# Attention in plain fp32 on half and quarter tiles of TensorE in place of split operands on whole tiles

## The chip, the cores and the metric

The kernel runs on one core of a Trainium2 chip. That core has TensorE (PE in the profile, PEld for its weight loads), VectorE (DVE), ScalarE (ACT), GpSimd (POOL) and SyncE (SP, which issues DMAs). The metric is the device time of one execution in microseconds. Before the change it is 808.48 us, the median of 3 runs.

## The reference

Attention with rotary embedding over 2 batches of 8 heads, 576 tokens, 64 numbers per head, and behind it a gated feed-forward layer and a mixture of four experts on the 1152 tokens. Everything is fp32.

```python
q_rot, k_rot = (rotate(q), rotate(k))          # [2, 8, 576, 64]
scores = matmul(q_rot, k_rot.T) / sqrt(64)
attn = exp(scores - max(scores)); attn = attn / (sum(attn) + 1e-09)
x = matmul(attn, v)                            # -> [1152, 512]
xn = x / sqrt(mean(x * x) + 1e-06) * rms_g
g, val = xn @ w_gate, xn @ w_val               # 512 -> 1536
x = (silu(g) * val) @ w_out                    # 1536 -> 512
out = sum over 4 experts of p[:, e] * (relu(x @ w1[e]) @ w2[e])   # 512 -> 1024 -> 512
```

## The kernel before

**Operands.** The fast matmul type of the program is float32r. So that nothing is lost, each fp32 operand is held as a rounded part and a remainder ("hi" and "lo"), and a product is made of the parts that matter: three passes in the layers behind attention (PASSES), and in attention by stacking hi and lo on the 128 partitions, since a head has only 64 numbers.

**Stages.** Attention runs over 8 pairs of heads, pairs 0 to 3 for the first batch and 4 to 7 for the second. Then come the gate and value products (L805), the output product (L868), and for each expert its first layer (w1_unit, L931) and second layer (w2_group, L964).

**One pair.** Queries and keys are loaded and rotated (rotate, L446 to L452), split (split_hi, split_lo L500, v_hi, v_lo) and transposed on PE (q_or_k L525, k_left L535, q_left L547), with an evacuation of each transpose out of PSUM (evac, L511 to L515). s_tile makes the scores of 128 queries of one head against 576 keys: four float32r matmuls of 288 columns (L577), nine such steps in a pair (the ninth takes the 64 left-over queries of both heads, with eight matmuls). top takes the maximum on DVE (L583), expo the exponential on ACT (L588). t_tile, t_left, t_keys and t_corner transpose the exponentials on PE (L613, L629, L622, L636); parts evacuates each twice, hi on ACT (L606) and lo on DVE (L607). pv multiplies with the values: nine matmuls of 288 columns for each head and half of the queries (L652), folded over two halves of the partitions (L179 on ACT, L660 on DVE). scale_main and scale_left (L686, L697) divide by the sums.

**Around it.** The weights of the later layers are loaded, joined and split during pairs 4 to 7 (w_first, w_join L328 and L329, w_parts L368 and L369). gv_early makes gate and value products of the first batch while attention of the second is running: 16 groups of twelve matmuls, one PSUM bank each. The norm of the first batch (rms_mean L732, five plain fp32 matmuls a call; rms_spread L767; rms_apply) stands in pair 5.

**What sets the order.** The kernel is recorded, not scheduled: each step has a place, 9 for a pair plus a number from the tables POS, POS0, POSB, POS1 (and an engine from ENG and its like), and run() issues all steps sorted by place. Each engine then works through its own instructions in that order. PSUM has two buffers of two banks for scores ("big") and four of one bank for the rest ("one").

Of the kernel before, what the change touches and what calls it, by code (L numbers as in the profile page):

```python
# [8 lines left out]
F32 = mybir.dt.float32  # L9
# [12 lines left out]
    "load_k": -14.3442, "load_q": -13.3903, "rot_k0": -12.4, "rot_q0": -8.066,  # L22
    "rot_k1": -12.39, "rot_q1": -8.056, "rot_k2": -12.38, "rot_q2": -8.046, "rot_k3": -12.37, "rot_q3": -8.036,
    "sqadd": 15.77, "k_hi": -6.2198, "k_lo": -5.49, "q_hi": -5.473, "q_hi2": -4.604, "q_lo": -4.48, "kA": -3.592,
    "kLA": -4.0692, "qA0": -1.45, "qA1": -2.3793, "qB0": 1.5567, "qB1": 0.1894, "qL": 1.9708, "kB": 2.3,
    "kLB": 2.35, "qk_evac": 0.0223, "load_v": -3.3, "v_hi": 4.5018, "v_lo": 5.5461, "S": 0.1146, "top": 0.0456,
    "exp": 1.0525, "T": 2.2, "T_left": 7.9119, "T_corner": 6.2219, "T_keysA": 6.2256, "T_keysB": 11.3022,
    "hi": 0.0135, "lo": 0.8261, "pvA0": 8.9935, "pvA1": 9.4029, "pvB0": 12.6577, "pvB1": 13.5, "fold1": 0.2017,
    "fold2": 0.7357, "recip": 12.2577, "spread": 13.4482, "scale": 15.3215, "scale_left": 14.2785,
    "scale2": 0.0703, "squares": 15.7612, "mean": 1.3, "rspread": 4.8093, "apply": 5.5685,  # L30
    "apply_hi": 0.3766, "apply_lo": 0.5069,
    "w_first": [37.0005, 39.9382, 43.081, 45.3845, 48.8978, 50.7319, 54.1549, 55.9597, 79.06, 82.6],
    "w_join": [37.4505, 40.3882, 43.5310, 45.8345, 49.3478, 51.1819, 54.6049, 56.4097, 79.08, 82.7],
    "w_parts": [39.7348, 41.4602, 45.9122, 47.5214, 51.0007, 53.2283, 56.7202, 57.6825],
# [13 lines left out]
    "T_left": 7.9259, "pvA1": 9.8703, "T_corner": 5.9941,  # L48
    "gv_out": 0.2708, "lo": 0.4192, "recip": 11.4284, "pvB0": 13.0091,
}  # L50

POSB = {
# [3 lines left out]
}  # L56
ENGB = {"rot_k0": "v", "rot_k1": "v", "rot_k2": "v", "rot_k3": "v"}
POS7 = {
   
}  # L60
# [35 lines left out]
def attention_moe_kernel(ctx, tc, q, k, v, w_gate, w_val, w_out, rms_g, probs, w1, w2, rope, out):  # L96
# [63 lines left out]
    def lookup(name, base, first, second, last):  # L160
# [5 lines left out]
        for t in tables if pair == 0 or pair >= NPAIR else [base]:  # L166
            if name in t:
                return t[name]
# [1077 lines left out]
```

## Time and profile before

| | us |
|---|---|
| median of 3 runs | 808.48 |
| lowest, highest | 808.05, 809.56 |
| span of the profiled execution | 806.9 |
| first score matmul (L577) starts | 10.17 |
| first matmul of the output product (L868) starts | 251.70 |

Up to 251.7 us the core does attention and the gate and value products of the first chunk; from there to the end it does the output product, the other chunks and the experts. The profile gives each engine's busy time; on PE a matmul's bar includes its latency and bars overlap, so what one matmul costs in a run is read from the start of one to the start of the next. The mean of a group of short instructions on ACT or DVE likewise contains latency that the next instruction overlaps.

### The profile page before, as it was taken

The page shows a single profiled execution, that of the slowest core. Times are in us where ns is not written, and L with a number is a line of the kernel's source. Part 1 is how long each engine was busy: PE and PEld are TensorE (multiplying, and loading weights), DVE is VectorE, ACT ScalarE, POOL GpSimd, SP SyncE. Part 2 cuts the span into 40 slices and gives each one's busy share as a digit, 9 for nine tenths or more (in the row PEclk, how much of TensorE's full clock was granted, in tenths as well). Part 3 has the DMA queues.
Part 4 walks back from the last instruction along what each step waited for, and adds up shares of the span by engine and source line. Part 5 has one row for each costly group of instructions (what it writes and reads, how often), then busy time and mean ns, then how long its engine had stood idle before and what let it go on. Part 6 is the DMA issues. An engine that isn't in the chain of part 4 may idle for free.

```text
span 806.9 us, 13012 instructions
## 1 busy us (share of the span) xinstructions
PE 780.0 (97%) x4994; PEld 732.7 (91%) x4994; DVE 475.5 (59%) x883; ACT 397.5 (49%) x784; POOL 400.5 (50%) x320
## 2 busy tenths in 40 slices
PE   7899988899999999999999999999999999999997
PEld 6799877799998999999999899898989989898996
DVE  6899988977778765621286445445444444444442
ACT  4899988788565554213344334243333424333330
POOL 5777886672100066414436455555554555555440
PEclk9899999899999999999999999999999999999999
DMA  4011322230134433300000020110202011020002
GB/s 127 18 48 47 99 82 84 84 96 1 54 105 132 131 103 107 105 1 27 26 28 27 27 79 27 52 54 26 79 2 79 27 53 53 27 79 1 1 27 91
DMA packets 41805, 46.64 MB, mean 58 GB/s; under 512 B 7568, under 2 KB 34960, under 8 KB 41744
## 3 DMA queue, kind: packets, MB, share of 16 engines
q1 hardware_dynamic: 41744, 45.82, 18.3%
q8 instruction: 39, 0.64, 0.3%
q14 instruction: 22, 0.18, 0.1%
HBM read 43.45 MB, written 2.36 MB: 57 GB/s over the span
## 4 chain that ended last, share of the span: by engine, by line
PE 82%; DVE 7%; ACT 6%; issue 2%; POOL 1%; SPq 0%; DMA 0%; ACTq 0%; DVEq 0%; POOLq 0%
PE o L964 24%; PE o L931 22%; PE b L805 12%; PE o L868 9%; PE b L577 3%; PE o L652 3%; PE o L525 2%; PE o L613 2%; PE o L805 2%; ACT PP L588 1%; ACT PTA L606 1%; PE o L622 1%; DVE PTA L607 1%; ACT AR L179 1%; DVE nm L583 1%
## 5 line engine op out<-in xcount | busy, mean ns | idle before, releaser
L951 POOL TENSOR_TENSOR PTA<-PP,PTA 128x1152 fp32r<-128x1152 f32 x32 | 85.9, 2684 | 101.3 <-ACT PP L950 100.8
L964 PE MATMUL o<-QK,PTA 128*128 128x512 f32 x513 | 128.4, 389 | 0.0
L805 PE MATMUL b<-XN,WS 128*128 128x384 f32 (+1 forms) x768 | 126.5, 325 | 0.9 <-DVE PP L817 0.7
L805 PEld LDWEIGHTS b<-XN,WS 128*128 128x128 f32 x768 | 125.4, 188 | 1.5 <-DVE PP L817 1.3
L964 PEld LDWEIGHTS o<-QK,PTA 128*128 128x128 f32 x513 | 96.1, 188 | 19.8
L931 PE MATMUL o<-XN,WS 128*128 128x288 f32 x768 | 112.2, 295 | 0.0
L931 PEld LDWEIGHTS o<-XN,WS 128*128 128x128 f32 x768 | 105.7, 188 | 0.5
L384 POOL TENSOR_TENSOR WS<-RAW,WS 128x512 fp32r<-128x512 f32 x64 | 72.9, 1167 | 39.6 <-ACT WS L383 37.0
L949 ACT ACTIVATE PTA<-PP 128x1152 fp32r<-128x1152 f32 x32 | 37.4, 1168 | 106.2 <-DVE PP L944 106.2
L820 POOL TENSOR_TENSOR PTA<-PP,PTA 128x384 fp32r<-128x384 f32 x24 | 29.8, 1240 | 118.7 <-ACT PTA L819 118.7
L931 PE MATMUL o<-XT,WS 128*128 128x288 f32 x576 | 86.6, 295 | 0.0
L972 DVE SCALAR_TENSOR_TENSOR X<-o,pr,X 128x512 f32<-128x512 f32 x63 | 46.7, 749 | 64.9 <-PE o L964 64.9
L931 PEld LDWEIGHTS o<-XT,WS 128*128 128x128 f32 x576 | 79.8, 188 | 0.0
L383 ACT ACTIVATE WS<-RAW 128x512 fp32r<-128x512 f32 x64 | 32.5, 566 | 79.2 <-DVE RAW L391 79.2
L868 PE MATMUL o<-PTA,QK 128*128 128x288 f32 (+1 forms) x396 | 64.1, 305 | 0.8 <-ACT X L873 0.8
L607 DVE TENSOR_TENSOR PTA<-o,PTA 128x512 fp32r<-128x512 f32 (+2 forms) x96 | 61.3, 648 | 4.9 <-ACT PTA L606 3.9
L868 PEld LDWEIGHTS o<-PTA,QK 128*128 128x128 f32 x396 | 58.8, 188 | 1.0 <-ACT X L873 1.0
L583 DVE TENSOR_REDUCE nm<-b 128x1 f32<-128x576 f32 x72 | 54.1, 751 | 9.6 <-PE b L577 8.7
L606 ACT ACTIVATE PTA<-o 128x512 fp32r<-128x512 f32 (+2 forms) x96 | 53.5, 567 | 7.3 <-PE o L629 2.1
L937 DVE TENSOR_TENSOR PP<-o,PP 128x288 f32<-128x288 f32 x32 | 14.6, 457 | 71.9 <-ACT PP L936 65.6
L588 ACT ACTIVATE PP<-b,nm 128x576 f32<-128x576 f32 x72 | 53.4, 742 | 4.9 <-DVE nm L583 4.5
L817 DVE TENSOR_TENSOR PP<-b,PP 128x384 f32<-128x384 f32 (+1 forms) x32 | 17.0, 531 | 64.3 <-ACT PP L816 64.2
(184 smaller groups left out, 1449.3 us busy)
## 6 DMA issues: line engine op xcount, KB each, us to landing
RAW<-in_moe_w_dram SPq DMA_DIRECT2D x16, 512.0 KB, 3.4
AR<-in_moe_w_dram SPq DMA_DIRECT2D x16, 512.0 KB, 3.6
RAW<-in_moe_w_gate_dram SPq DMA_DIRECT2D x6, 512.0 KB, 3.5
RAW<-in_moe_w_val_dram SPq DMA_DIRECT2D x6, 512.0 KB, 3.4
AR<-in_moe_w_out_dram SPq DMA_DIRECT2D x6, 512.0 KB, 3.6
AR<-in_moe_w_gate_dram SPq DMA_DIRECT2D x5, 512.0 KB, 3.5
AR<-in_moe_w_val_dram SPq DMA_DIRECT2D x5, 512.0 KB, 3.4
AR<-in_v_dram SPq DMA_DIRECT2D x8, 256.0 KB, 3.4
```

What stands on the lines that cost most here:

```text
L384: eng.tensor_sub(dst(1), src, f32(dst(0)))
L583: nc.vector.tensor_reduce(nm[:, bufi, j : j + 1], box[0][:, :, 0:HS], axis=AX.XY, op=ALU.max, negate=True)
L588: nc.scalar.activation(pp(pair, j).rearrange("p (n t) -> p n t", n=2), box[0][:, :, 0:HS], AF.Exp, bias=nm[:, bufi, j : j + 1], scale=1.0, ...
L606: at(time + when("hi"), lambda: nc.scalar.activation(hi, view(box[0]), AF.Copy))
L607: at(time + when("lo"), lambda: nc.vector.tensor_sub(lo, view(box[0]), f32(hi)))
L805: nc.tensor.matmul(ps[:, 0:n], lhsT=w[:, lw, d, :], rhs=XN[:, lx, d, tok], start=(i == 0), stop=(i == 3 * ND - 1))
L868: nc.tensor.matmul(ps[:, 0:n], lhsT=w[:, lw, d * P : (d + 1) * P], rhs=hb(f, lx, tok), start=(i == 0), stop=(i == 11))
L931: nc.tensor.matmul(ps, lhsT=w[:, lw, a, k, :], rhs=xs(b, lx, k, c), start=(i == 0), stop=(i == 5))
L949: nc.scalar.activation(hi, q, AF.Relu)
L951: nc.gpsimd.tensor_sub(lo, q, f32(hi))
L964: nc.tensor.matmul(ps, lhsT=hb(f, lx, slice(t * P, (t + 1) * P)), rhs=w[:, lw, :], start=(i == 0), stop=(i == 11),)
L972: nc.vector.scalar_tensor_tensor(OA[:, t, :], in0=ps, scalar=p, in1=OA[:, t, :], op0=ALU.mult, op1=ALU.add)
```

## The change

Attention is done in plain fp32. Nothing is split: split_hi, split_lo, q_again, v_parts, the tiles QK, V2, QLZ and both evacuations of parts are gone.

- turn transposes the rotated keys or queries of both heads of a pair, in ten transposes of 64 partitions each, with one evacuation. Afterwards one head stands on partitions 0 to 63 and the other on 64 to 127 (KQ), and two DMAs from SBUF to SBUF (dup) write each head to the other half too (KQ2).
- s_step makes the scores of 128 queries of one head in two matmuls of 288 columns, one on each half of the partitions (left-over queries: four, on quarters). In the first two steps of pair 0 both heads are done at once from KQ alone.
- t_tile transposes in 8 or 10 pieces of 64 partitions and evacuates once (evac, mostly ACT); t_left has three evacuations.
- pv works on quarters of the array: 64 keys by 64 numbers of a head, 18 matmuls for both heads of one half of the queries, in three places (two, two and one key chunks). The two halves of the keys land in two banks, added by pv_out on ACT and pv_add on DVE.
- PSUM: "two" and "acc" are single buffers of two banks (transposes of the exponentials in the one; turn, pv, scale and gv_early in the other) until turn_over, after the last pair, swaps them for four buffers of one bank.
- gv_early evacuates gate and value together. The rope table is loaded from the ACT queue. All places in the tables are new.

```diff
 POS = {
-    "load_k": -14.3442, "load_q": -13.3903, "rot_k0": -12.4, "rot_q0": -8.066,
+    "load_k": -12.18, "load_q": -12.0135, "load_v": -0.6939, "rot_k0": -10.5625, "rot_k1": -9.0157, "rot_k2": -8.4013,
...
+    def turn(time, pair, m, eng):
+        x = turned[m]
...
+            box.append(ps_two(acc))
+            for i in range(5):
+                for r in range(2):
+                    a = HALF[r]
...
+                    nc.tensor.transpose(box[0][:, 1 - r, c : c + 64], x[a, o : o + P], ident[a, a])
...
+            nc.sync.dma_start(out=y[HALF[1], o : o + a.stop - a.start], in_=x[HALF[0], a])
+            nc.sync.dma_start(out=y[HALF[0], b], in_=x[HALF[1], b])
...
+            for n in range(2):
+                for i in (h,) if t < 4 else range(2):
+                    rows, c = (slice(0, P), cols) if t < 4 else (HALF[i], slice(576 - 576 * i, 640 - 576 * i))
                     nc.tensor.matmul(
-                        box[0][:, n, 0:HS], lhsT=lhsT, rhs=QKV[:, 2, h, cols],
-                        start=(i == 0), stop=(i == len(todo) - 1),
+                        box[0][rows, n, 0:HS], lhsT=queries(pair, i, c, n == i), rhs=keys(pair, i, n, n == i),
+                        start=True, stop=True,
                     )
...
+    def t_tile(time, pair, h, t, eng):
...
+            box.append(ps_two())
+            for i in range(nk):
+                for r in range(2):
+                    a, o = HALF[r], (ks.start + i) * P
+                    nc.tensor.transpose(box[0][:, r, 64 * i : 64 * i + 64], pp(pair, t)[a, o : o + P], ident[a, a])
...
-        at(time + when("hi"), lambda: nc.scalar.activation(hi, view(box[0]), AF.Copy))
-        at(time + when("lo"), lambda: nc.vector.tensor_sub(lo, view(box[0]), f32(hi)))
...
+            for k in ks:
+                for h in range(2):
+                    for r in range(2) if k < 4 else (h,):
+                        i = 4 if k == 4 else 5 * h + k
+                        nc.tensor.matmul(
+                            box[0][HALF[h], r, 0:HS], lhsT=VN[HALF[r], pair % 2, i, :],
+                            rhs=PT[pair % 2][HALF[r], i, cols], start=(k == 0), stop=(k == (4 if h == r else 3)),
+                        )
```

On PE, about the middle of an early pair, it stood before like this (L577 scores, L613 and L629 transposes of exponentials, L525 of queries and keys, L652 the value product):

```order
L577 MATMUL b_670<-QK 128x288 x4
L613 MATMUL o_677<-ident,PP 128x128 x4
L525 MATMUL o_683<-ident,XN 128x128 x4
L629 MATMUL o_689<-ident,PP 128x128 x4
L577 MATMUL b_696<-QK 128x288 x4
L613 MATMUL o_703<-ident,PP 128x128 x4
L652 MATMUL o_710<-PTA,V_70 128x288 x9
```

It stands now like this (L549 scores from KQ and the copy KQ_80, L578 and L596 transposes of exponentials, L619 the value product, L494 turn):

```order
L549 MATMUL b_935<-KQ_80 128x288
L549 MATMUL b_935<-KQ 128x288
L596 MATMUL t_940<-ident,PP 128x64 x10
L619 MATMUL t_956<-PTX,VN 64x288 x8
L549 MATMUL b_965<-KQ 128x288
L549 MATMUL b_965<-KQ_80 128x288
L578 MATMUL t_969<-ident,PP 128x64 x8
L619 MATMUL t_956<-PTX,VN 64x288 x10
L549 MATMUL b_996<-KQ_80 128x288
L549 MATMUL b_996<-KQ 128x288
L578 MATMUL t_1001<-ident,PP 128x64 x10
L494 MATMUL t_1016<-ident,AR 128x64 x10
```

A score step went from four matmuls to two, the transposes from whole blocks to twice as many of half their columns, and the value product of both heads and one half of the queries is cut in pieces that stand between score steps.

On PE at the end of attention it stood before like this (L805 gate and value products, L686 and L697 the scaling):

```order
L652 MATMUL o_2603<-PTA,V_70 128x288 x9
L613 MATMUL o_2616<-ident,PP 128x128 x4
L622 MATMUL o_2623<-ident,PP 64x128 x4
L805 MATMUL o_2629<-XN,WS 128x288 x12
L652 MATMUL o_2644<-PTA,V_70 128x288 x9
L652 MATMUL o_2660<-PTA,V_70 128x288 x9
L686 MATMUL o_2672<-ident,AR_76 128x128 x4
```

And now (L767 gate and value products, L655 the scaling):

```order
L578 MATMUL t_2291<-ident,PP 128x64 x8
L767 MATMUL t_2302<-XN,WS 128x288 x24
L578 MATMUL t_2333<-ident,PP 128x64 x10
L619 MATMUL t_2344<-PTX,VN 64x288 x16
L596 MATMUL t_2361<-ident,PP 128x64 x10
L619 MATMUL t_2344<-PTX,VN 64x288 x2
L619 MATMUL t_2381<-PTX,VN 64x288 x18
L655 MATMUL b_2417<-ident,AR_82 128x64 x8
```

Of the gate and value products of the first batch, 9 of 16 groups of twelve stood before the last value product; now 6 of 16 do (three blocks of 24), and the rest follows behind it.

On SP the copies stand between the loads (L505 and L506 the copies, L425 and L430 loads of queries or keys, L460 and L463 of values):

```order
L432 DMA AR<-in_k_dram 128x2x256
L437 DMA AR<-in_k_dram 64x64 x2
L432 DMA AR<-in_q_dram 128x2x256
L437 DMA AR<-in_q_dram 64x64 x2
L457 DMA AR<-in_v_dram 128x2x256
L462 DMA AR<-in_v_dram 64x2x64 x2
```

and now

```order
L505 DMA KQ_80<-KQ 64x288
L506 DMA KQ_80<-KQ 64x288
L425 DMA AR<-in_k_dram 128x2x256
L430 DMA AR<-in_k_dram 64x64 x2
L505 DMA KQ_80<-KQ 64x576
L506 DMA KQ_80<-KQ 64x576
L425 DMA AR<-in_q_dram 128x2x256
L430 DMA AR<-in_q_dram 64x64 x2
L460 DMA VN<-in_v_dram 128x256
L463 DMA VN<-in_v_dram 64x64
```

Four copies for each pair came into this queue, and each stands behind whatever load was recorded ahead of it.

## Rows read from the trace of the kernel before

**Rows 1.** The page's first part: busy us, share of the span, instructions of each engine.

```profile
PE 780.0 (97%) x4994; PEld 732.7 (91%) x4994; DVE 475.5 (59%) x883; ACT 397.5 (49%) x784; POOL 400.5 (50%) x320
```

**Rows 2.** Busy time by stretch, all engines; the first line names the columns.

```profile
core 0: us, PE busy (x) PEld busy (x) DVE busy (x) ACT busy (x) POOL busy (x), PEclk, DMA share, GB/s
10.20:33.90 23.70, 18.02 (x110) 15.72 (x111) 17.49 (x27) 16.80 (x44) 18.83 (x20) 0.86 0.26 66
54.90:74.30 19.40, 19.26 (x155) 18.55 (x155) 18.14 (x34) 18.44 (x45) 13.30 (x15) 1.00 0.17 49
74.30:94.10 19.80, 19.63 (x156) 18.55 (x155) 18.69 (x34) 19.04 (x46) 17.20 (x18) 1.00 0.33 99
119.90:152.30 32.40, 26.16 (x172) 23.38 (x171) 28.11 (x60) 25.06 (x58) 19.65 (x20) 0.84 0.24 78
214.00:251.70 37.70, 36.00 (x266) 34.98 (x265) 30.21 (x70) 22.08 (x52) 3.21 (x4) 1.00 0.28 87
251.70:806.90 555.20, 550.30 (x3314) 515.79 (x3312) 268.76 (x484) 199.79 (x324) 257.38 (x172) 1.00 0.16 51
```

**Rows 3.** The chain that ended last, in order: start us, us, what.

```profile
258.98 19.49 PE o L868 x144
428.71 22.26 PE o L931 x168
778.29 24.52 PE o L964 x108
```

**Rows 4.** Groups on PE by shape: count | busy us, mean ns | idle before.

```profile
L577 PE MATMUL b<-QK 128*128 128x288 f32 x256 | 50.2, 320 | 2.3 <-ACT PP L588 1.9 <-DVE QK L515 0.3
L577 PE MATMUL b<-QK,QLZ 128*128 128x288 f32 x64 | 10.9, 316 | 0.0
L652 PE MATMUL o<-PTA,V 128*128 128x288 f32 x288 | 45.7, 303 | 0.2
L613 PE MATMUL o<-ident,PP 128*128 128x128 f32 x256 | 40.3, 281 | 2.6 <-DVE RAW L329 2.2 <-DVE X L689 0.2
L525 PE MATMUL o<-ident,XN 128*128 128x128 f32 x192 | 30.8, 293 | 2.8 <-DVE PTA L607 1.5 <-ACT QK L511 0.5 <-DVE X L702 0.4
L636 PE MATMUL o<-ident,PP 128*64 128x128 f32 x8 | 2.3, 292 | 0.5 <-ACT PP L588 0.5
L805 PE MATMUL o<-XN,WS 128*128 128x288 f32 x192 | 28.5, 300 | 0.8 <-DVE AR L660 0.6 <-ACT AR L773 0.2
L805 PE MATMUL b<-XN,WS 128*128 128x288 f32 x192 | 26.3, 296 | 0.9 <-DVE PP L817 0.7
```

**Rows 5.** Timeline on PE, stretches 8 to 10 and 124 to 127: start us, us.

```profile
8.25 1.47 PE L525 MATMUL o<-ident,XN 128*128 128x128 f32 x12
9.46 0.14 PEld L535 LDWEIGHTS o<-ident,XN 128*128 128x128 f32 x1
9.56 0.27 PE L535 MATMUL o<-ident,XN 128*128 128x128 f32 x1
...
124.69 1.17 PEld L732 LDWEIGHTS o<-ones,AR 128*128 128x128 f32 x10 [0.48 <-issue]
125.88 0.20 PEld L547 LDWEIGHTS o<-ident,XN 128*128 128x128 f32 x2
```

**Rows 6.** Timeline on PE, stretch 137 to 139: a change of tile shape.

```profile
137.59 0.85 PE L767 MATMUL o<-ident,st 128*128 128x128 f32 x5 [1.69 <-ACT QK L511]
138.16 0.13 PEld L767 LDWEIGHTS o<-ident,st 64*128 64x128 f32 x1 [0.17 <-issue]
```

**Rows 7.** Groups on DVE and ACT by shape, columns as in rows 4.

```profile
L607 DVE TENSOR_TENSOR PTA<-o,PTA 128x512 fp32r<-128x512 f32 x72 | 48.7, 681 | 4.2 <-ACT PTA L606 3.7
L606 ACT ACTIVATE PTA<-o 128x512 fp32r<-128x512 f32 x72 | 42.8, 595 | 4.3 <-PE o L629 2.1 <-PE o L613 1.6
```

**Rows 8.** Who waited for whom, PE, stretch 94 to 166: us, times, longest.

```profile
PE o L613 <- DVE RAW L329: 2.2, 3, 1.0
```

**Rows 9.** DMA issues: count, KB each, median us from issue to landing.

```profile
AR<-in_v_dram SPq DMA_DIRECT2D x16, 32.0 KB, 3.0
```

More of the change, by code (lines that the diff above doesn't have):

```diff
@@ new lines, in dup @@
+        def dup():
+            x = KQ[:, pair % 2, m, :]
+            y = KQ2[:, pair % 2, HS * m : HS + 640 * m]
+            b, a = (slice(0, S), slice(64, 640)) if m else (slice(0, HS), slice(352, 640))
+            o = a.start if m else 0
+            nc.sync.dma_start(out=y[HALF[1], o : o + a.stop - a.start], in_=x[HALF[0], a])
+            nc.sync.dma_start(out=y[HALF[0], b], in_=x[HALF[1], b])
+        at(time, mm)
+        at(time + when("kq_evac"), out)
+        at(time + when("dup"), dup)
@@ new lines, in keys, with queries, pp, s_step @@
+    def keys(pair, h, n, own):
+        if own:
+            o = 64 - 64 * h + n * HS
+            return KQ[HALF[h], pair % 2, 0, o : o + HS]
+        return KQ2[HALF[1 - h], pair % 2, 0:HS]
+    def queries(pair, h, cols, own):
+        if own:
+            return KQ[HALF[h], pair % 2, 1, cols]
+        return KQ2[HALF[1 - h], pair % 2, HS + cols.start : HS + cols.stop]
+    def pp(pair, step):
+        o = 1152 * ((5 * pair + step) % 3)
+        return PPf[:, o : o + 1152]
+    def s_step(time, pair, t, h, both):
+        buf = pair % 2
+        j = 4 * h + t if t < 4 else 8
+        cols = slice(64 + t * P, 64 + (t + 1) * P)
@@ L558, in attention_moe_kernel @@
[L558 to L567 removed]
+            if both is not None:
+                if h == 0:
+                    both.extend([ps_big(), ps_big()])
+                    for n in range(2):
+                        for i in range(2):
+                            nc.tensor.matmul(
+                                both[i][:, n, 0:HS], lhsT=queries(pair, i, cols, True), rhs=keys(pair, i, n, True),
+                                start=True, stop=True,
+                            )
+                box.append(both[h])
+                return
@@ L634, in t_corner @@
[L634 to L645 removed]
+        ks = slice(4, 9) if h else slice(0, 4)
@@ L646, in pv, with t_left @@
+        at(time, mm)
+        at(time + when("T_out"), out)
+    def t_left(time, pair, engs):
         box = []
         def mm():
-            todo = [(kt, hl) for kt in range(4) for hl in range(2)] + [(4, 0)]
-            box.append(ps_one())
-            for i, (kt, hl) in enumerate(todo):
-                nc.tensor.matmul(
-                    box[0][:, 0:HS], lhsT=V2[:, 5 * h + kt, :],
-                    rhs=PT[:, kt, hl, h, cols] if kt < 4 else PT4[:, h, cols],
-                    start=(i == 0), stop=(i == 8),
-                )
@@ L658, in pv @@
-        at(time, mm)
-        at(time + when("fold1"), lambda: copy(fold, tt[a, cols], box[0][z, 0:HS]))
-        at(time + when("fold2"), lambda: nc.vector.tensor_add(yy[a, cols], box[0][a, 0:HS], tt[a, cols]))
+            box.append(ps_two())
+            for k in range(5):
+                for r in range(2):
+                    a = HALF[r]
+                    o = 64 + P * k + 64 * r if k < 4 else 576 * (1 - r)
+                    nc.tensor.transpose(box[0][:, r, 64 * k : 64 * k + 64], pp(pair, 4)[a, o : o + P], ident[a, a])
@@ new lines, in attention_pair @@
+        at(t0 + when("load_v"), load_v, pair)
+        for t in range(5):
+            both = [] if pair == 0 and t < 2 else None
+            for h in range(2) if t < 4 else (0,):
+                s_step(t0 + when("S") + 2 * t + h, pair, t, h, both)
+        for t in range(4):
+            t_tile(t0 + 2 * t + when("TA"), pair, 0, t, eng[f"TA{t}"])
+            t_tile(t0 + 2 * t + 1 + when("TB"), pair, 1, t, eng[f"TB{t}"])
+        t_left(t0 + when("T_left"), pair, [eng[f"left{i}"] for i in range(3)])
```

433 lines of the change are left out of this document (175 added, 258 removed), and 46 rows, old and new, of tables (ENG, ENG0, ENG1, ENGL).

## The prediction

> **What bounds the kernel now.** I read the chain of waits first. From 258.98 us to the end it is PE alone, piece after piece of float32r matmuls [rows 3], and in the stretch from 251.7 PE is busy 550 of 555 us [rows 2]. The change touches nothing there, so these 555.2 us stay, and the question is what becomes of the first 251.7 us. A busy PE is not yet a full one (its bars overlap, and 97% over the span [rows 1] says little), so I price its work by runs. 168 float32r matmuls of 288 columns take 22.26 us [rows 3], 0.1325 us each. Twelve transposes of 128 columns take 1.47 us, the last bar being about 0.27 long [rows 5]; eleven steps in 1.20 us are 0.109 us each.
>
> A pair has (256 + 64 + 288) / 8 = 76 matmuls [rows 4], 10.1 us, and 78 transposes (624 in nine groups, of which the largest two and the smallest stand in [rows 4]), 8.5 us: 18.6 us of PE. Pairs 2 and 3 take 19.4 and 19.8 us, and in them DVE, ACT and PE are all over 90% busy [rows 2]. So a steady pair is bound by PE, with 1.0 us of stall, and ACT and DVE are close behind. The sum to 251.7: start 10.2; eight pairs 148.8; 32 groups of twelve gate and value matmuls [rows 4] 50.9; some 3 for norm and scaling; what is left, 39 us, is stall. Most of it lies in pair 0 and in pairs 4 to 6, where weights are prepared: the stretch from 119.9 to 152.3 has PE busy 26 of 32 us, DVE 28, the clock at 0.84 [rows 2], and transposes wait for the weight joins on DVE [rows 8].
>
> **The change, part by part.** *ACT, DVE, POOL.* The remainder of every transposed block goes (on DVE 48.7 us for the main form alone, 6.1 a pair [rows 7]), with it the splits of queries, keys and values; eight folding steps on half the partitions become four on all. The hi evacuation on ACT [rows 7] stays as the only one, in blocks of 512 and 640 columns. I put ACT at some 13 us a pair and DVE at some 10, against 18 to 19 now [rows 2]. Both fall well under PE: what they lose is gained only as stall that PE no longer has.
>
> *PE, price of a plain fp32 matmul.* No row shows one of this width, so I build it. The five plain fp32 products of the norm appear as ten weight loads [rows 5]: each product is two instructions. Moving a plain fp32 column costs 0.109 / 128 = 0.85 ns, against 0.46 for float32r. One instruction of 288 columns is then 0.245 us, a product 0.49 us. A weight load of such a product is (1.17 - 0.19) / 9 = 0.109 us for 128 columns, 0.055 for 64; that of a transpose 0.06, the distance of two in [rows 5] (0.20 less one of 0.14).
>
> A pair has now 20 score products, 36 value products and 112 half transposes of 64 columns. What they cost depends on how far instructions on different parts of the array run at once, and no row shows two parts at work. The bounds: nothing at once gives 9.8 + 17.6 + 6.7 = 34.1 us; everything at once (scores and transposes two at a time, values four) gives 4.9 + 4.4 + 3.1 = 12.4 us. I take this: matmuls on different parts stream together, since the order rows alternate the parts instruction by instruction, but weight loads come one after the other, since wherever loads stand in a run in this trace they follow each other at the distance of a full load [rows 5]. Loads then cost 40 x 0.109 = 4.4 for scores, 72 x 0.055 = 4.0 for values, 112 x 0.06 = 6.7 for transposes. The larger of load and stream counts: 4.9 + 4.4 + 6.7 = 16.0 us.
>
> *Changes of tile shape.* Around the one transpose on half the rows, PE needs some 0.1 us more than in a run, before it (idle 0.17 ahead of the load) and behind it [rows 6]. Values and left-over scores are on quarters, all else on halves: four value pieces and one score step, in and out, 10 x 0.1 = 1.0 us a pair. Together 17.0 us a pair, against 18.6.
>
> *Stalls.* Single buffers for the transposes and for the values mean that each transpose block waits for the evacuation of the one before it. A block takes 0.5 to 0.6 us on PE, 0.27 to land, 0.6 on ACT [rows 7]: 1.5 us, nine times 13.5 us a pair, under 17; a score step and a value piece lie between. I keep 1.0 us a pair, as in pairs 2 and 3, and 10 us more for the start, the pair with the norm and the tail, in place of 39 - 8 = 31. At the far end, had the weight preparation stalled PE as it does now, 21 us would come back.
>
> *Moves at no cost.* Six of the gate and value groups instead of nine before the last value product: PE is full either way, and behind attention they cover the norm of the second batch. Four copies a pair on SP: the nearest row is a small load, 3.0 us to landing [rows 9]; they are issued about three score steps (5 us) ahead of use, so hidden; without that cover up to 3 us at the head of seven pairs, 21 us. The table on the ACT queue: start unchanged within a microsecond or two.
>
> *Sum.* 10.2 + 8 x 17.0 + 50.9 + 3 + 8 + 10 = 218.1 us instead of 251.7: 33.6 less. On the profiled execution's 806.9 that is 773.3; the median of the runs lies 1.6 us above the span, so **775 us**. Break-even is at 17.0 + 33.6 / 8 = 21.2 us of PE a pair.
>
> **The rivals.**
>
> *Strict order (the slower one).* The two instructions of one product stand side by side on the same part of the array. If matmuls start only in program order, the second waits for the first, and what follows, though on another part, waits behind it: only the second half of one product and the first of the next run together. A score step is then three passes of 0.245 us, 8 x 0.74 = 5.9, the left-over step five, 1.2; value pieces of 8 and 10 products are 9 and 11 passes, 40 a pair, 9.8 us. With 6.7 for transposes and 1.0 for shapes that is 24.6 us a pair, 7.6 more than I take: 775 + 61 = 836 us. If weight loads for the two halves come side by side, transposes are 3.1 and the pair is 21.0: 807 us, just at break-even. It turns slower than before from the 21.2 us a pair of the break-even. For it: the two loads of a product do stand one behind the other, ten for five products [rows 5]. Against it: nothing in this trace, which never uses two parts at once.
>
> The Trainium skill (TensorE: Matmul & The Clock Gate, Part 3, The mechanism) says that matmuls on different tiles overlap, starting some 4 ns apart, and that they keep program order in start and in end. The first half is the forecast's overlap, the second half speaks for this rival; it tells nothing of fp32 products made of two instructions, and no run here shows either.
>
> *Everything at once.* If loads too come side by side, PE needs 12.4 + 1.0 = 13.4 us a pair and ACT, at some 13, and the single transpose buffer, at 13.5, become the bound; with a little stall I take 16 instead of 18 a pair: 775 - 16 = 759 us.
>
> *It doesn't do what it says.* The parts don't run at once: 35.1 us a pair, 775 + 145 = 920 us. No row speaks for or against it; the price alone keeps it out of the range.
>
> *Copies late.* As above, 775 + 21 = 796 us.
>
> **How the numbers follow.** Forecast (765 to 788) 0.47; everything at once (752 to 765) 0.12; strict order with loads side by side (797 to 817) 0.18; strict order with loads in line (817 to 845) 0.17; no overlap 0.03; copies late 0.03. The two sides of strict order meet near the old time: of its 0.18 I put 0.08 faster, 0.05 within 0.2% (about what a measurement of this kernel can tell from no change), 0.05 slower. Faster: 0.47 + 0.12 + 0.03 + 0.08 = 0.70; same 0.05; slower 0.05 + 0.17 + 0.03 = 0.25. The range leaves out the lower end of the second case (some 0.04) and the upper two thirds of the fourth with no overlap (0.14): 755 to 825 us.
>
> **What the profile after would show.** A steady pair, from one first score matmul to the next, 18 us by the forecast, 16 if everything overlaps, 22 to 26 under strict order, over 35 with none. A value piece of eight products: 1.0 us by the forecast from first to last start, 2.2 under strict order, 3.9 without overlap. A block of ten half transposes: 0.6 us if loads come in line, 0.3 if side by side. DVE and ACT at 10 and 13 us a pair; the output product starting at 218 us. Wrong would be a matmul of 288 plain columns that is not 0.245 us, a clock that falls in attention, or score matmuls that wait for the copies; and if PE's first output product came much later than 219 us with pairs at 18, the gate and value products behind attention would be waiting for something.

## The result, and the profile after

The changed kernel takes 795.77 us (median of 4 runs, 794.63 to 796.85), the kernel before in the same session 808.98 us (808.05 to 809.56). The ratio is 0.9836 with a 95% interval of 0.9822 to 0.985: faster, by 13 us or 1.6%, which is clear of the scatter of the runs. The forecast was 775 us, a gain of 33.5. The sign was right and the time lies in the range, but most of the expected gain is missing.

The first part of the page of the changed kernel (engine, busy us, share of the span, instructions), to be read beside [rows 1]:

```profile
PE 754.4 (95%) x5554; PEld 661.5 (83%) x5554; DVE 428.9 (54%) x791; ACT 345.7 (44%) x642; POOL 356.6 (45%) x284
```

Every engine has less to do, PE by 26 us and DVE by 47, and the span fell by 14 only. The loss has a place. This is the busy time by stretch in the changed kernel, columns as in [rows 2]; each of the eight middle rows runs from the first score matmul of a pair to that of the next, the last pair's to the first output product (L832), and the last row is what stands behind it:

```profile
core 0: us, PE busy (x) PEld busy (x) DVE busy (x) ACT busy (x) POOL busy (x), PEclk, DMA share, GB/s
0.00:11.65 11.65, 7.55 (x57) 6.93 (x57) 6.88 (x21) 1.99 (x2) 4.78 (x15) 1.00 0.44 118
11.65:26.84 15.19, 12.08 (x123) 8.23 (x123) 7.65 (x11) 10.06 (x24) 9.19 (x10) 0.78 0.54 125
26.84:44.65 17.81, 15.93 (x224) 10.21 (x225) 11.55 (x24) 13.72 (x32) 8.40 (x9) 1.00 0.33 86
44.65:62.19 17.54, 15.94 (x224) 10.18 (x224) 10.88 (x19) 14.15 (x32) 13.78 (x16) 1.00 0.37 94
62.19:79.09 16.90, 15.91 (x225) 10.24 (x225) 10.76 (x19) 14.07 (x32) 11.46 (x13) 1.00 0.37 100
79.09:98.87 19.78, 16.97 (x225) 9.91 (x225) 14.70 (x26) 16.72 (x37) 14.28 (x15) 1.00 0.47 136
98.87:127.45 28.58, 21.57 (x241) 13.31 (x240) 24.54 (x52) 17.80 (x37) 13.81 (x13) 0.88 0.39 109
127.45:157.18 29.73, 22.36 (x251) 13.78 (x250) 23.33 (x35) 18.30 (x39) 17.39 (x15) 0.89 0.42 124
157.18:234.56 77.38, 73.52 (x682) 62.79 (x682) 50.43 (x109) 38.95 (x84) 5.79 (x7) 1.00 0.16 50
234.56:792.90 558.34, 552.56 (x3314) 515.94 (x3312) 268.18 (x484) 199.94 (x324) 257.69 (x172) 1.00 0.17 51
```

Pairs 1 to 3 take 17.8, 17.5 and 16.9 us; pairs 2 and 3 took 19.4 and 19.8 before [rows 2]. That is the forecast's 18, and a little better. But pairs 5 and 6 take 28.6 and 29.7 us (3.2 of the latter are 24 gate and value products), and in them DVE is busy 24.5 and 23.3 us against 11 in a steady pair. In these two pairs six of the eight weights of pairs 4 to 6 are joined from their two words, and the first batch is normalised. The output product starts at 234.6 us, where the forecast had 218.1, and the part behind it takes 558.3 us instead of 555.2 [rows 2].

What a wait looks like there is seen in the timeline of the changed kernel from 131.9 to 137.7 us, PE, DVE and POOL (start us, us, engine, line, operation, then in brackets the idle time ahead and who ended it):

```profile
132.08 1.17 DVE L748 SCALAR_TENSOR_TENSOR X<-X,g_sb 128x576 f32<-128x576 f32 x1
...
132.42 0.76 PE L549 MATMUL b<-KQ 64*128 64x288 f32 x4 [0.37 <-ACT PP L559]
132.71 1.80 POOL L444 TENSOR_TENSOR AR<-AR,X 128x576 f32<-128x576 f32 x1
...
133.17 1.89 DVE L321 SCALAR_TENSOR_TENSOR RAW<-RAW 128x512 int32<-128x512 int32 x1
135.09 0.69 DVE L322 SCALAR_TENSOR_TENSOR RAW<-RAW 128x512 int32<-128x512 int32 x1
135.70 0.75 DVE L555 TENSOR_REDUCE nm<-b 128x1 f32<-128x576 f32 x1
136.37 1.07 DVE L475 COPY PTX<-t 128x320 f32<-128x320 f32 x3
...
137.59 0.37 PE L578 MATMUL t<-ident,PP 64*128 64x64 f32 x2 [4.41 <-DVE PTX L475]
```

PE ends a score step at 133.18 and then stands for 4.41 us. Its next transposes need the single buffer "two", which is free when DVE has evacuated the left-over block (L475). That evacuation, and the maximum of the scores just made (L555), stand in DVE's queue behind a scaling of the norm (L748) and two join instructions (L321, L322). No piece of this is long; PE pays for their row. PE stands for 14.4 us in pairs 5 and 6. Its two largest waits there (who, for whom, us in total, times, longest):

```profile
PE t L578 <- DVE PTX L475: 5.2, 2, 4.4
PE b L549 <- ACT PP L559: 5.1, 5, 2.1
```

### The profile page after: what moved, and what is told of

Its sections match the earlier page's. It is cut to its first block, busy times and chain, and to the rows that moved or that the text cites. A ratio compares the mean times of both kernels' runs of the same rounds, so it can differ in the third digit from the quotient of the medians.

```text
span 792.9 us, 13873 instructions
## 1 busy us (share of the span) xinstructions
PE 754.4 (95%) x5554; PEld 661.5 (83%) x5554; DVE 428.9 (54%) x791; ACT 345.7 (44%) x642; POOL 356.6 (45%) x284
## 3 DMA queue, kind: packets, MB, share of 16 engines
q1 hardware_dynamic: 42576, 48.66, 20.8%
## 4 chain that ended last, share of the span: by engine, by line
PE 82%; DVE 9%; ACT 4%; POOL 2%; issue 2%; DMA 1%; ACTq 0%; POOLq 0%; DVEq 0%
PE o L928 25%; PE o L895 22%; PE b L767 14%; PE o L832 9%; PE t L619 5%; PE b L549 2%; PE t L578 1%; PE t L767 1%; DVE nm L555 1%; ACT PP L559 1%; POOL AR L444 1%; DVE RAW L321 1%; POOL AR L453 1%; DVE X L660 1%; ACT PTX L473 1%
## 5 line engine op out<-in xcount | busy, mean ns | idle before, releaser
L928 PE MATMUL o<-WL,HB 128*128 128x512 f32 x675 | 165.1, 391 | 0.0
L928 PEld LDWEIGHTS o<-WL,HB 128*128 128x128 f32 x675 | 126.4, 188 | 27.2
L767 PE MATMUL b<-XN,WS 128*128 128x384 f32 (+1 forms) x888 | 143.2, 321 | 1.8 <-DVE XN L752 1.4
L767 PEld LDWEIGHTS b<-XN,WS 128*128 128x128 f32 x888 | 141.4, 188 | 2.7 <-DVE XN L752 1.9
L915 POOL TENSOR_TENSOR HB<-PP,HB 128x1152 fp32r<-128x1152 f32 x32 | 86.1, 2691 | 100.8 <-ACT PP L914 100.3
L782 POOL TENSOR_TENSOR HB<-PP,HB 128x384 fp32r<-128x384 f32 x24 | 29.8, 1241 | 124.1 <-ACT HB L781 124.1
L913 ACT ACTIVATE HB<-PP 128x1152 fp32r<-128x1152 f32 x32 | 37.3, 1167 | 106.2 <-DVE PP L908 106.2
L832 PE MATMUL o<-HB,WL 128*128 128x288 f32 (+1 forms) x528 | 76.8, 306 | 2.0 <-DVE PP L779 1.2
L832 PEld LDWEIGHTS o<-HB,WL 128*128 128x128 f32 x528 | 76.0, 188 | 2.6 <-DVE PP L779 1.6
L555 DVE TENSOR_REDUCE nm<-b 128x1 f32<-128x576 f32 x72 | 53.8, 749 | 30.8 <-PE b L549 26.7
L549 PE MATMUL b<-KQ 64*128 64x288 f32 (+1 forms) x304 | 52.3, 452 | 9.8 <-ACT PP L559 9.3
L928 PE MATMUL o<-WS,HB 128*128 128x512 f32 x189 | 54.1, 394 | 0.0
```

The lines of the kernel that those rows point to most:

```text
L549: nc.tensor.matmul(box[0][rows, n, 0:HS], lhsT=queries(pair, i, c, n == i), rhs=keys(pair, i, n, n == i), start=True, stop=True,)
L555: nc.vector.tensor_reduce(nm[:, buf, j : j + 1], box[0][:, :, 0:HS], axis=AX.XY, op=ALU.max, negate=True)
L767: nc.tensor.matmul(ps[:, 0:n], lhsT=w[:, lw, d, :], rhs=XN[:, lx, d, tok], start=(i == 0), stop=(i == 3 * ND - 1))
L832: nc.tensor.matmul(ps[:, 0:n], lhsT=w[:, lw, d * P : (d + 1) * P], rhs=hb(f, lx, tok), start=(i == 0), stop=(i == 11))
L913: nc.scalar.activation(hi, q, AF.Relu)
L915: nc.gpsimd.tensor_sub(lo, q, f32(hi))
```

## The experiments

The theory behind them: DVE's in-order queue, filled in pairs 4 to 6 with joins and norm that the change left as they were, holds up the maxima and evacuations that PE needs, so the stalls that I expected to vanish stayed. Rivals: the loop of scores, maxima and buffers is slow of itself; PE's work or the order on the array is dearer than read; the low clock.

### Joins left out, in both kernels

```diff
+        if joins[0]:   # False during attention
             eng.tensor_scalar(b.bitcast(I32), b.bitcast(U32), 2.0**-29, 7.0, ...)
...
+        if joins[0]:
             nc.vector.scalar_tensor_tensor(bi, in0=si, scalar=-(2**31), in1=bi, ...)
             nc.vector.scalar_tensor_tensor(ai, in0=si, scalar=3, in1=bi, ...)
```

> The changed kernel without the three DVE instructions (L314, L321, L322) that join the two words of a weight, for the ten weights prepared during attention; those weights are then wrong numbers, all other work stays. Theory DVE queue: pairs 5 and 6 last 28.6 and 29.7 us because these joins (14.5 us of DVE in the stretch 98.87 to 157.18) stand in one queue with the maxima and evacuations for which PE waits. Without them the two pairs fall to some 20 us each: 775 to 781 us. Rival score chain: the pairs are held by maximum, exponential and single buffers, whatever else DVE does: at most 5 us less, 791 to 796 us. Rival clock: the half-clock stretch in each of the two pairs stays, and with it most of the loss: 788 to 792 us.

> The kernel before with the same joins left out (L321, L328, L329, ten weights). If the joins were a floor under pairs 5 and 6 in both kernels, this one gains as much as the changed one does, 14 to 20 us: 789 to 795 us, and the difference between the two kernels without joins is about the 13 us it is with them. If PE's 18.6 us of work a pair covered most of the joins before and the change laid them bare, the gain here is under 8 us, 801 to 807 us, and the two kernels without joins lie 20 us or more apart.

Without joins the changed kernel takes 785.19 us (ratio to before 0.9709, 0.9694 to 0.9723) and the kernel before 797.86 (0.9864, 0.9849 to 0.9879). Each gains 10.6 us on its own median. So the joins are on the path in both kernels at the same price, and the gap between the kernels is as wide without them as with them: the change as a whole left this price where it was. Both times lie between the ranges that I had given for the theory and for its rivals, so joins are a good part of the excess and not the whole: pairs 4 to 6 of the changed kernel fall from 78.1 us to 69.2, where three steady pairs and 3.2 us of gate and value products would be 55.4.

```profile
79.51:99.25 19.74, 16.74 (x224) 9.82 (x225) 10.71 (x19) 16.54 (x37) 13.97 (x15) 1.00 0.54 156
99.25:123.54 24.29, 20.10 (x241) 12.02 (x240) 16.24 (x41) 17.35 (x37) 12.94 (x14) 0.93 0.44 124
123.54:148.66 25.12, 20.28 (x250) 12.92 (x250) 18.49 (x29) 18.14 (x39) 17.43 (x15) 1.00 0.50 147
```

Those are pairs 4, 5 and 6 of the changed kernel without joins, columns as above. The low clock comes with the waits: the granted clock of pairs 5 and 6 is 0.88 and 0.89 with joins, 0.93 and 1.00 here. In pair 5 with joins it stood at its lower level, 1.2 GHz, from 108.2 to 115.0 us, with PE busy all that time, and just ahead of that, from 103 to 108 us, PE had been busy 1.4 us in all.

So the clock is no cause beside the waits, but it is much of their price. Of the 8.9 us that pairs 4 to 6 lose with the joins, 3.8 are PE's busy time (60.9 to 57.1) and the rest is PE standing. In the kernel before, by the borders of [rows 2], the three stretches from 94.1 to 180.6 us fall from 86.5 to 77.5, and of these 9.0 us 5.8 are PE's busy time (75.4 to 69.7); its clock there goes from 0.93, 0.84 and 1.00 to 1.00 in all three.

### The norm's DVE work left out too, then the rest of the preparation

```diff
+            if b == 0:
+                nc.vector.tensor_copy(r_, m)
+                return
...
-        at(time, scale)
+        if b:
+            at(time, scale)
```

and for the second kernel, on top, no scaled copy on ACT and parts of 8 columns:

```diff
+            y, lo8 = x[:, 0:8], slot[:, 512:520]
+            nc.scalar.activation(slot[:, 0:8], y, AF.Copy)
+            eng.tensor_sub(lo8, y, f32(slot[:, 0:8]))
...
+        nc.vector.memset(f32(WS[:, 0:4, :]), 0.5)
+        nc.gpsimd.memset(f32(WS[:, 4:8, :]), 0.5)
```

> The changed kernel without the joins (as in no_joins) and also without DVE's part of the norm of the first batch: the reciprocal root (some 15 small instructions) and the four scalings L748 (4.6 us); one copy stands for the root, and the results are wrong. If weights and norm on DVE together make the whole excess of pairs 5 and 6 over a steady pair (40.8 us over 35): both pairs come to 17.5 to 18.5 us and the total to 776 to 780 us. If something else holds them (POOL's rotation, ACT, half clock): the pairs stay over 20 us and the total over 781 us.

> The kernel of no_joins_norm without the rest of the weight preparation in attention as well: no scaled copy on ACT (L313), and the two parts of a weight (ACT L361, POOL L362) made for 8 of 512 columns; the slots are filled with a constant at the start, and the results are wrong. Loads stay. If the preparation of weights and the norm are the whole excess of pairs 4 to 6 over a steady pair: pairs 4, 5 and 6 (less its gate and value products) come to 17.2 to 18.5 us each, and the total to 771 to 775 us, which is what the forecast said for a change whose stalls were hidden. If the loop of scores, maxima and buffers is slower there for another reason (clock, copies, order of the tables): they stay at 20 to 21 us and the total at 778 to 781 us.

Without joins and norm: 781.04 us (ratio 0.9658, 0.964 to 0.9677). Without the rest of the preparation as well: 779.81 us (0.9648, 0.9629 to 0.9667), of which 1.7 us are the constant written at the start (the first score matmul stands at 13.3 us instead of 11.6). Without joins and norm, pairs 5 and 6 take 21.5 us and 24.1 (20.9 without the gate and value products), not the 17.5 to 18.5 of the theory: that was the sign that something else holds them too. Pairs 4 to 6 of the one without preparation, columns as above:

```profile
81.45:100.14 18.69, 16.47 (x224) 9.78 (x225) 10.66 (x19) 13.96 (x34) 11.77 (x15) 1.00 0.53 151
100.14:121.21 21.07, 18.30 (x239) 11.45 (x240) 13.63 (x28) 14.09 (x34) 10.06 (x14) 1.00 0.49 140
121.21:143.02 21.81, 20.06 (x250) 12.93 (x249) 13.44 (x25) 16.04 (x37) 12.91 (x15) 1.00 0.58 169
```

The three pairs come to 61.6 us, by way of 69.2 without joins and 65.3 without joins and norm. Of the 22.7 us by which pairs 4 to 6 of the changed kernel exceed three steady pairs (78.1 less 55.4), taken off in this order, the joins make 8.9, the norm's DVE work 3.8, the ACT and POOL work on weights 3.8, and 6.2 stay. My expectation for the last kernel, 771 to 775 us, was missed by some 3 us once the start is taken off, and the total lies in the other range, 778 to 781: preparation is most of the excess and not all of it. Pair 5 is still at 21.1 us, 3.7 over a steady pair, and that is the norm's own work on PE, which no kernel here left out (PE in pair 5 without preparation; us busy, mean ns, idle time ahead; L703 is rms_mean, L742 rms_spread):

```profile
L703 PE MATMUL t<-ones,AR 128*128 128x1 f32 x8 | 1.0, 249 | 0.8 <-ACT WS L371 0.8
L742 PE MATMUL t<-ident,st 128*128 128x128 f32 x4 | 0.6, 285 | 0.7 <-ACT PTX L483 0.7
```

With their three instructions of a smaller shape (0.6 us) the two are busy 2.2 us, and PE stands 1.5 us ahead of them. The other 2.5 of the 6.2 us, in pairs 4 and 6, stay open.

### The same work in other places

Three kernels leave nothing out and only move the weight preparation. The first spreads it over pairs 1 to 4, where DVE is busy 11 of 17.5 us:

```diff
-    "w_first": [37.3773, 39.157, 43.081, 45.3845, 48.8978, 50.7319, 54.1549, 55.6932, ...
+    "w_first": [11.0, 15.5, 20.0, 24.5, 29.0, 33.5, 38.0, 42.5, ...
```

(`w_join` and `w_parts` one and two units later, the loads from 6.5.)

> The changed kernel with the preparation of the first eight weights moved from pairs 4 to 6 to pairs 1 to 4, where DVE is 62 to 65% busy. Nothing is left out. Theory DVE queue: pairs 5 and 6 fall by 12 to 18 us together, pairs 1 to 4 grow by at most 1 us each: 779 to 787 us. Rival score chain or clock: nothing is gained in pairs 5 and 6, and ACT (14 us of 17.5 busy) makes pairs 1 to 4 longer: 795 to 800 us.

802.56 us (ratio 0.9919, 0.9902 to 0.9936): 6.8 us slower than the changed kernel, where the theory had 779 to 787 us and its rivals 795 to 800. Pairs 5 and 6 did fall, from 58.3 to 50.0 us. But pairs 1 to 4 rose from 72.0 to 87.5, nearly 2 us for each weight, though no engine is full there:

```profile
28.52:50.64 22.12, 18.47 (x225) 11.79 (x225) 15.54 (x27) 15.81 (x35) 10.79 (x10) 0.85 0.49 146
50.64:71.51 20.87, 16.07 (x224) 10.26 (x224) 15.63 (x25) 16.43 (x36) 17.24 (x18) 1.00 0.37 102
```

DVE is busy 15.5 of 22.1 and 15.6 of 20.9 us, and PE waits all the same (pairs 1 to 4):

```profile
PE t L494 <- DVE KQ L475: 4.2, 2, 2.5
PE t L578 <- ACT PTX L473: 3.1, 5, 0.8
PE t L494 <- DVE AR L627: 3.1, 1, 3.1
PE t L494 <- POOL AR L453: 2.9, 1, 2.9
```

So the theory has to be put otherwise. It is not that DVE has no time left. Preparation put into a queue delays what stands behind it, and in a pair PE soon waits for that, on a single buffer or a maximum. Free time of DVE, summed over a pair, took up little of that here. Two things besides DVE belong to the 15.4 us. The ACT and POOL work on the weights moved along with the joins, and some of the waits end there. And the clock fell in pairs 1 and 3, to 0.85 and 0.86: PE's busy time in the four pairs rose from 64.8 to 70.4 us.

The other two move weights the other way, into pair 7 and behind it, where gate and value products give PE other work:

```diff
-    "w_first": [..., 45.3845, 48.8978, 50.7319, 54.1549, 55.6932, ...
+    "w_first": [..., 45.3845, 58.6, 61.5, 64.5, 67.0, ...
```

> The changed kernel with the preparation of weights 5 to 8 moved from pairs 5 and 6 into pair 7, where DVE is busy 15.5 of 30.3 us and POOL 2.2, and gate and value products fill PE. Nothing is left out. If joins cost what they cost because DVE's queue stands ahead of PE's single buffers and maxima in a pair without spare PE work, and nothing where PE has other work queued: pairs 5 and 6 fall by 4 to 6 us together, pair 7 grows by at most 2: 790 to 793 us. If a join costs the same wherever it stands (as it did in pairs 1 to 4): 795 to 798 us.

```diff
-    "w_first": [37.3773, 39.157, 43.081, 45.3845, 48.8978, 50.7319, 54.1549, 55.6932, ...
+    "w_first": [37.3773, 39.157, 58.6, 61.0, 64.0, 66.5, 69.0, 71.5, ...
...
-            gv_early(POS["gv"][2 * i : 2 * i + 2], i % 4, i // 4)
+            gv_early(POS["gv"][2 * i : 2 * i + 2], i // 2, i % 2)
```

> The changed kernel with the preparation of weights 3 to 8 in pair 7 and behind it, and the early gate and value groups in the order chunk by chunk, both halves of the tokens of one before the next, so that late weights are in time. Nothing is left out. If what late_w gained (2.9 us for four weights) goes on for two more: 790 to 792 us. If pair 7's queue of DVE is full by then and the gate and value products wait for weights: 793 to 797 us.

The second also takes the gate and value products chunk by chunk, so that late weights are in time; this new order was not run by itself. Four weights late: 792.94 us (ratio 0.9805, 0.9786 to 0.9823), inside the expected 790 to 793. Six weights late: 788.83 us (0.9756, 0.9735 to 0.9778), below both kernels, and lower than I expected. Pairs 4 to 6 and the stretch from pair 7 to the output product with six late weights:

```profile
79.59:99.41 19.82, 16.98 (x225) 9.91 (x225) 13.90 (x25) 16.18 (x36) 14.19 (x15) 1.00 0.48 136
99.41:121.38 21.97, 18.74 (x240) 11.68 (x241) 15.27 (x41) 13.69 (x30) 9.48 (x11) 1.00 0.30 76
121.38:146.71 25.33, 20.27 (x250) 12.92 (x249) 22.04 (x35) 18.44 (x39) 14.30 (x13) 1.00 0.24 66
146.71:228.08 81.37, 75.26 (x683) 63.25 (x683) 57.39 (x122) 43.75 (x92) 14.28 (x13) 0.98 0.29 90
```

The three pairs fall by 11.0 us and the last stretch grows by 4.0. The same preparation costs about a third where PE has other products to run. Of the 11.0 us 4.9 are PE's busy time (60.9 to 56.0), with the clock at 1.00 in all three pairs.

### One part of the change alone: where the scaled word lies

The change also flips one flag that I had passed over: the scaled high word of a weight no longer goes to PSUM during attention, so the first join reads two operands in SBUF. Here that is done to the kernel before.

```diff
-    scaled, in_psum = [], [True]
+    scaled, in_psum = [], [False]
```

> The kernel before with one part of the change alone: the scaled high word of a weight is kept in SBUF and not in PSUM, so that the first join instruction reads two operands in SBUF. In the changed kernel these instructions take 0.68 us where POOL is idle and 1.0 to 1.9 us beside POOL work; in the kernel before, with one operand in PSUM, 0.69 us in either case. Theory DVE queue: 3 to 6 us more DVE time where DVE is the bound, 811 to 815 us. If the place of the operand costs nothing at the end: 808 to 810 us.

810.97 us, ratio 1.0032 (1.0021 to 1.0044): some 2.5 us slower, a little under the 3 to 6 us expected. The joins of pairs 4 to 6 by group, of the kernel before and of this one (mean ns in the next to last number):

```profile
L329 DVE SCALAR_TENSOR_TENSOR RAW<-o,RAW 128x512 int32<-128x512 int32 x8 | 5.5, 691 | 0.7
L328 DVE SCALAR_TENSOR_TENSOR RAW<-o,RAW 128x512 int32<-128x512 int32 x8 | 5.5, 685 | 1.7 <-ACT o L320 1.6
```

```profile
L329 DVE SCALAR_TENSOR_TENSOR RAW<-RAW 128x512 int32<-128x512 int32 x8 | 9.7, 1218 | 0.3
L328 DVE SCALAR_TENSOR_TENSOR RAW<-RAW 128x512 int32<-128x512 int32 x8 | 7.8, 975 | 0.5 <-ACT RAW L320 0.3
```

With one operand in PSUM a join takes 0.69 us whether POOL works or not. With both in SBUF it takes 0.69 where POOL is idle and up to 1.78 beside it. In the changed kernel the 1.89 us of the join in the timeline above, beside a 1.80 us POOL instruction, is the same thing. It also means that the equal 10.6 us of the two kernels is in part chance: from this kernel to the one before without joins it is 13.1 us, so with like operands the joins may have become some 2.5 us cheaper with the rest of the change, and the flag took that back. No run shows this directly.

### PE and ACT in a steady pair

Half of the key chunks of the value product left out:

```diff
             for k in ks:
+                if k in (2, 3):
+                    continue
```

> The changed kernel without the value products of key chunks 2 and 3 (16 of 36 products a pair; the attention output is then wrong). A piece of eight products takes 1.13 us on PE (distance in the trace), so PE has 2.3 us less in each pair, all else stays. If PE still sets the steady pairs, as the forecast had it: pairs 1 to 3 fall from 17.4 to 15.0 to 15.5 us, and the total to 776 to 782 us. If the queue of DVE and ACT and the single buffers set them: pairs 1 to 3 stay within 0.7 us, total 789 to 796 us.

788.46 us (ratio 0.9754, 0.9731 to 0.9776). Pairs 1 to 3 take 16.5, 18.7 and 16.2 us, together 0.8 us less than the 52.2 of the changed kernel, for 6.9 us less of PE by the price of a piece. Pair 2 is no fair case, since its clock fell to 0.91; at full clock pairs 1 and 3 gain 1.3 and 0.7 us for 2.3 each. That lies between the two branches of the expectation, nearer to the second: the steady pair is no longer set by PE alone. Most of the 7 us stems from elsewhere, 3.1 from pairs 4 to 6 and 3.5 from pair 7 to the output product. PE's waits in these pairs are now for the rotation on POOL and for the exponentials (L494 is the turn of keys or queries, L549 the scores; pairs 1 to 4):

```profile
PE t L494 <- POOL AR L453: 4.7, 5, 1.8
PE b L549 <- ACT PP L559: 4.2, 7, 0.8
```

Four evacuations of a pair taken from ACT and given to DVE, in pairs 1 to 3:

```diff
-    "TA0": "a", "TA1": "a", "TA2": "a", "TA3": "a", "TB0": "a", ...
+    "TA0": "v", "TA1": "v", "TA2": "v", "TA3": "v", "TB0": "a", ...
```

> The changed kernel with the four evacuations of 512 columns of exponentials of a pair on DVE instead of ACT, in pairs 1 to 3 alone: ACT some 2.4 us less, DVE some 2.0 us more. If ACT's load sets the steady pair (14 us busy of 17.4): pairs 1 to 3 fall by 0.5 to 1.5 us each, total 791 to 794 us. If PE does: within 0.3 us a pair. If each microsecond put into DVE's queue delays PE, as with the joins in pairs 1 to 4 (15.4 us for 8 of them): 1 to 2 us more a pair, 798 to 802 us.

796.15 us (ratio 0.9845, 0.9829 to 0.986), no difference at the end that the intervals show. The pairs take 18.1, 17.9 and 17.6 us, 0.3 to 0.7 longer. ACT, at 14 of 17.4 us, is not what holds a pair, and some 2 us more on DVE cost about a fifth of themselves here, much less than a join did. A likely reason, not tested, is that an evacuation that only changes its engine holds up nothing new.

### The order on the array

The value products of a piece tile after tile, and the half transposes half after half, same instructions:

```diff
-            for k in ks:
-                for h in range(2):
-                    for r in range(2) if k < 4 else (h,):
+            for h in range(2):
+                for r in range(2):
+                    for k in [k for k in ks if k < 4 or r == h]:
```

```diff
-            for i in range(nk):
-                for r in range(2):
+            for r in range(2):
+                for i in range(nk):
```

> The changed kernel with the value products of a piece written tile after tile (both key chunks of one quarter, then the next quarter) where they alternate now; same instructions. Theory that quarters run at once whatever the order: a piece stays at 1.0 to 1.2 us, total 795 to 797 us. Rival, strict order of the forecast (an instruction starts only when the one ahead has started, and two on one quarter run one after the other): a piece of eight products is 13 passes of 0.245 us, 3.2 us instead of 1.1, 8 us more a pair, 850 to 865 us.

> The changed kernel with all half transposes written half after half (five in a row on one half of the rows, then five on the other) where the halves alternate now; same instructions. As the quarters of the value product did, the halves should find each other over a row of five: ten stay at 0.3 us from first to last start, total 795 to 797 us. In strict order ten take 0.6 us, nine blocks and three others a pair, 8 x 12 x 0.3 us of PE, of which PE's waits hide half: 805 to 825 us.

Tile after tile: 795.46 us (ratio 0.9837, 0.9818 to 0.9857), the same as alternating. A piece of eight products on PE, in the changed kernel and in this one, and the start of the latter seen through a window of 0.1 us:

```profile
65.03 1.20 PE L619 MATMUL t<-PTX,VN 64*64 64x288 f32 x16
```

```profile
65.63 1.22 PE L619 MATMUL t<-PTX,VN 64*64 64x288 f32 x16
...
65.63 0.49 PE L619 MATMUL t<-PTX,VN 64*64 64x288 f32 x4
```

Sixteen passes take as long as before, and four of them start within 0.1 us though the program has four passes of one quarter in a row. For the quarters strict order is refuted. Half after half: 799.1 us (0.9877, 0.9857 to 0.9896), 3.3 us slower, between the two ranges expected. Ten transposes take 0.58 us where they took 0.47, some 0.1 us a block, so the array does look past a row of five, but not for nothing; the strict case would have cost 0.3 a block. The block of ten of this kernel on PE, beside 0.47 us in the dense run shown further below:

```profile
72.54 0.58 PE L578 MATMUL t<-ident,PP 64*128 64x64 f32 x10
```

## Why the prediction was wrong, step by step

**The sum.** Taken apart in the forecast's own terms, the time to the first output product is 11.65 us of start, 8 x 15.9 of PE, 50.9 of gate and value products, 3 of norm and scaling, and the rest, 41.8, stall: 234.6. The forecast had 10.2 + 8 x 17.0 + 50.9 + 3 + 18 = 218.1. Start was 1.45 too low, PE 8.8 too high, and stall 23.8 too low. Behind it come 3.1 us that I had excluded, and the median lies 2.9 above the span instead of 1.6. Together 20.8 us, the distance from 775 to 795.8. By place, and before the 3 us for norm and scaling are taken off, the stall lies with 4.5 us in pairs 1 to 3, 27.2 in pairs 4 to 6 and 13.1 in pair 0 and from pair 7 on.

**The step that failed is the stall term.** "I keep 1.0 us a pair ... and 10 us more for the start, the pair with the norm and the tail, in place of 39 - 8 = 31." Stall was 39 us before by this reckoning and is 42 now. I had seen where it lay ("pairs 4 to 6, where weights are prepared", with transposes waiting for the joins [rows 8]), and took it to vanish because DVE, relieved of the remainders, would be far under PE. DVE did fall, to 11 us a steady pair. The kernels without joins show what became of the stall: the same 10.6 us in both. And the weights moved to pairs 1 to 4 show why free DVE time doesn't take it up: single buffers and maxima make PE wait for the queue, not for the sum. The sentence for the far end, "had the weight preparation stalled PE as it does now, 21 us would come back", names what happened, and I gave it no chance of its own. That its 796 us meet the measured 795.8 is luck: the stall was 23.8 us over, and PE's price, the start and the end make up the difference. Not all of the 27.2 us by which pairs 4 to 6 exceed PE's work is weights: 8.9 are joins, 7.6 the norm's DVE work and the other work on weights, 3.7 the norm's products on PE (for which the sum has its 3 us), 2.5 unexplained, and some 4.5 are the stall of any three pairs. Nor is all of it waiting: PE stands for 17.2 us of it, and 10.0 are busy time beyond the price of its work, at a granted clock of 0.88 and 0.89 in pairs 5 and 6. The forecast had the 0.84 of [rows 2] before it and no term for the clock.

**PE's price was near, for reasons that were partly wrong.** The plain fp32 product was right: passes on one quarter follow each other at 0.24 us. That loads come in line was wrong: ten half transposes start within 0.25 to 0.31 us, the rival's 0.3 for loads side by side. The value piece starts within 0.8 us where the forecast had 1.0. So everything overlaps, as in the rival that I gave 0.12. But its 13.4 us a pair were too few. A dense run in pair 3, PE, start us, us:

```profile
73.87 0.76 PE L549 MATMUL b<-KQ 64*128 64x288 f32 x4
74.46 0.41 PE L578 MATMUL t<-ident,PP 64*128 64x64 f32 x8
74.79 1.69 PE L619 MATMUL t<-PTX,VN 64*64 64x288 f32 x20
76.41 0.76 PE L549 MATMUL b<-KQ 64*128 64x288 f32 x4
77.00 0.47 PE L578 MATMUL t<-ident,PP 64*128 64x64 f32 x10
77.50 0.46 PE L655 MATMUL t<-ident,AR 64*128 64x64 f32 x8
77.80 0.22 PE L655 MATMUL t<-ident,rr 64*128 64x64 f32 x2
77.95 0.72 PE L549 MATMUL b<-KQ 64*64 64x288 f32 x8
78.59 0.28 PE L578 MATMUL t<-ident,PP 64*128 64x64 f32 x2
```

From start to next start a score step takes 0.59 us (0.49 by its passes), eight transposes 0.33, ten 0.45 to 0.5, a value piece of 20 passes 1.62. Each group costs 0.1 to 0.2 us beyond its passes, 25 times a pair, where I had counted ten changes of shape of 0.1. Eight score steps and the left-over one make 5.4, twelve blocks of transposes about 5, four value pieces 5.5: 15.9 us, which is also PE's busy time in pairs 1 to 3. The two errors nearly met, at 17.0.

**The steady pair** was forecast at 18 and came at 17.4 on average. The rival's 16 failed because of what each group costs beyond its passes, and because a lighter PE meets POOL's rotation and the exponentials, as the half value product showed.

**Strict order, no overlap, copies late.** The first two are refuted. The copies take 4.0 us to land and no wait of PE on them appears:

```profile
KQ<-KQ SPq DMA_DIRECT2D x16, 144.0 KB, 4.0
```

**ACT and DVE** at 13 and 10 us were forecast; 14.0 and 11.1 were found. Right enough, and no help.

**The sign to look for** in a late output product was wrong: I named gate and value products waiting behind attention. They wait 1.4 us. The lateness was in pairs 4 to 6. Another sign of being wrong did show, a clock that falls in attention: it was 0.88 and 0.89 in pairs 5 and 6, and 0.78 in pair 0.

**What I passed over**: the flag that took the scaled word out of PSUM. In the kernel before it costs some 2.5 us.

**Behind the output product** 3.1 us were lost. One piece is a wait of 1.2 us ahead of the last output products; in the second layer each of eight runs of 108 matmuls of 512 columns takes 24.54 to 24.81 us in the chain instead of the 24.50 to 24.52 before, 1.9 in all. The cause of the latter is open.

## What to carry to other kernels

A stall that the trace shows in one stage can belong to the work of that stage, and a change that doesn't touch this work then leaves it, however much it relieves the engine elsewhere: give it its own line in the sum, at its old price, before any gain. Free time on an in-order engine, summed over a stretch, says little of what another instruction in its queue costs; look who waits behind it, and whether that one has other work. A wait of PE can cost more than its own length: here the clock fell behind such waits, and about four tenths of what the joins cost in pairs 4 to 6 was PE working longer. Preparation that must be somewhere goes where the bounding engine has a long run of independent products, which here brought another 7 us.

## What the runs showed of the hardware

**Plain fp32 on parts of the array.** A product is two passes of 0.24 us for 288 columns, and passes on four quarters start about 0.01 us apart and run together in both orders tried, alternating and tile after tile. Transposes on halves, written five in a row, cost about 0.1 us more for a block of ten. The Trainium skill (TensorE: Matmul & The Clock Gate, Part 3, The mechanism) has starts some 4 ns apart, where this trace has 6 to 7 ns (13 to 14 tile after tile), and program order in start and end. With the latter it disagrees: written tile after tile, four passes started within 0.1 us, where passes of one quarter are 0.24 us apart.

**DVE beside POOL.** A DVE instruction of 512 columns with both operands in SBUF took 0.68 to 0.69 us alone and up to 1.89 beside POOL; with one operand in PSUM 0.69 in both cases. The Trainium skill (SBUF — State Buffer, section SBUF: two separate sides) says that a DVE operation with two SBUF inputs and a GpSimd operation that reads SBUF exclude each other for a whole instruction; the trace agrees, the join ending 0.55 us after the 1.80 us POOL instruction that started ahead of it.
